# Top-k attention with a leaky-ReLU MLP: values and the scores of two units grouped on TensorE, with the PSUM banks shared out anew

## The chip, the cores and the metric

The kernel runs on one core of a Trainium2 chip. The metric is the device time of one execution in microseconds (us); lower is better. The engines are called PE (TensorE matmul), PEld (TensorE weight load), DVE (VectorE), ACT (ScalarE), POOL (GpSimd) and SP (SyncE, which here only issues DMAs).

## The reference

A batch of 8, with 8 heads, 576 tokens and head size 64, goes through attention in which each query keeps only its 32 largest scores. The result is laid out as 4608 tokens of 512 numbers and goes through an MLP of width 2048 with a leaky ReLU. All is in float32.

```python
scores = scale * np.matmul(q, k.transpose(0, 1, 3, 2))          # (8, 8, 576, 576)
kth = np.partition(scores, -top_k, axis=-1)[..., -top_k:-top_k + 1]   # top_k = 32
scores = np.where(scores >= kth, scores, -1000000000.0)
attn = np.exp(scores - np.max(scores, axis=-1, keepdims=True))
attn = attn / (np.sum(attn, axis=-1, keepdims=True) + 1e-09)
x = np.matmul(attn, v).transpose(0, 2, 1, 3).reshape(8 * 576, 512)
h = x @ w_in                                                    # (512, 2048)
g = np.maximum(0.01 * h, h)
return g @ w_out                                                # (2048, 512)
```

## The kernel before

**Units.** Attention is cut into 144 units. A whole unit is 128 queries of a pair of heads; its tile of scores is 128 x 2 x 576, one row of 576 for each query and each head. The 64 queries that 576 leaves over after four times 128 are taken from two pairs at once (a left unit, two per batch). A pair's two heads lie in partitions 0 to 63 and 64 to 127 of `qt` and `kt`, so a scores matmul uses half of the rows of the array.

**Steps.** The program is a list of steps, and every engine runs its instructions in the order in which the steps write them (`tc.manual_schedule()`). In step s, unit s is in `top_k` on DVE (four rounds of MAX8 and MATCH_REPLACE8 on the halves' pairwise maxima and minima). Unit s - 1 is masked on POOL (`mask`) and goes through the exponential on ACT (`exponents`, then `sums`, tile `ze`). Unit s - 2 gets its reciprocal on DVE (`rz`, which needs `ze`), is normalized on ACT, split into 16-bit halves on ACT (`split`), written to DRAM (`apart`) and read back transposed by a DMA (`wT`, three buffers).

**The block.** At the end of every even step comes a block of attention on PE: `scores` of units s + 2 and s + 3 (line 191) and `weigh_values` of units s - 4 and s - 3 (line 276), with the copies out of PSUM on ACT (`s_sb`, line 207, and `x`, line 297). In the kernel before, the order is scores of the first new unit, values of the two old ones, scores of the second new unit:

```python
            for u in new[:1]:
                scores(u)
            if s % 2 == 0:
                po = ps_po.tile([P, 2, P], F32, name="po")
                ...
            for u in new[1:]:
                scores(u)
```

A unit's scores are four matmuls of 288 columns for a whole unit (two heads, two halves of the keys), eight for a left unit. They go to two PSUM tiles of two banks each, `psc0` for one head and `psc1` for the other, and there is one buffer of each.

**The MLP.** Between the blocks PE works on the MLP of finished tokens, in chunks of 256 (two of 128 at first). `mlp(ch)` is a generator: first 16 chunks f of the hidden width, each of four matmuls of 256 columns into a tile `ph` with a Prelu on ACT into `gT[f]` (lines 330 to 340); then, per 128 tokens, 16 matmuls of 512 columns into a tile `pz`, a copy to `o_sb` and the DMA out. Every `yield` names the cost of what was issued, and `mlp_steps(budget)` takes pieces until a seventh of the step's share of the backlog is used; there are seven such calls in a step. The two early chunks of 128 tokens take another way (`hidden_of_few`), with x as the weights and PE transposes (`pt`) afterwards.

**PSUM.** There are eight banks: two each for `psc0` and `psc1`, one for `po` (the values), three for the MLP's tiles (`ps_ml`, tag "ml").

**Start.** The MLP's weights come in 16 pieces as 64-bit numbers, and `round_weights` makes float32 of each from its 16-bit words, over ACT, DVE and PE. Its PE sums use `psc0` and `psc1` in turn, and the last three pieces the MLP's banks. For odd pieces the step that makes `scale` (line 127) is on ACT, for even ones on DVE (line 131). The scores of units 0 and 1 are issued while the last pieces are under way.

Of the kernel before, what the change touches and what calls it, by code (L numbers as in the profile page):

```python
# [8 lines left out]
F32 = mybir.dt.float32  # L9
# [10 lines left out]
def kernel(  # L20
# [13 lines left out]
    nc = tc.nc  # L34
# [9 lines left out]
    HP = DMODEL // P  # L44
    B = NPAIR // HP
    HS = S // 2
    NFC = DFF // P
    WCH = 1024
    LEFT = S % P
# [11 lines left out]
    small = ctx.enter_context(tc.tile_pool(name="small", bufs=5))  # L61
    halves = ctx.enter_context(tc.tile_pool(name="halves", bufs=3, space=bass.MemoryType.DRAM))
    ps_sc = ctx.enter_context(tc.tile_pool(name="ps_sc", bufs=1, space=bass.MemoryType.PSUM))
    ps_po = ctx.enter_context(tc.tile_pool(name="ps_po", bufs=1, space=bass.MemoryType.PSUM))
    ps_ml = ctx.enter_context(tc.tile_pool(name="ps_ml", bufs=3, space=bass.MemoryType.PSUM))

    ident = const.tile([P, P], F32, name="ident")
    make_identity(nc, ident)
# [4 lines left out]

    w_in = [const.tile([P, DFF], F32, name=f"w_in{c}") for c in range(HP)]
    w_out = [const.tile([P, 4, DMODEL], F32, name=f"w_out{c}") for c in range(NFC // 4)]
    gT = [const.tile([P, CHMAX], F32, name=f"gT{f}") for f in range(NFC)]

# [23 lines left out]
    def round_weights(n):  # L103

        raw = raw_of.pop(n)
        dst = piece(n)  # L110
        mid = raw[:, :, 2]
        low = raw.rearrange("p n w -> p (n w)").bitcast(U32).rearrange("p (n w) -> p n w", w=2)[:, :, 0]
        top = raws.tile([P, WCH], U16, name="top", bufs=2)
        scale = raws.tile([P, WCH], U16, name="scale", bufs=2)
        parts = work.tile([P, 2 * NKC - 1, P], F32, name="wT", bufs=3)
        parts = parts.rearrange("p c n -> p (c n)").bitcast(U16)
        m_top, m_low = parts[:, 0:WCH], parts[:, WCH:2 * WCH].bitcast(BF16)
        nc.scalar.copy(top, raw[:, :, 3])
        nc.scalar.activation(dst, mid, AF.Copy, bias=-7.0 - 2.0 ** -16, scale=2.0 ** -20)

        nc.scalar.activation(m_low, low, AF.Copy, bias=128.0, scale=2.0 ** -29)  # L121
        yield
        nc.vector.tensor_scalar(scale, top, 4, 0x7FF, ALU.logical_shift_right, ALU.bitwise_and)

        nc.vector.tensor_scalar(scale, scale, 1151.0, 896.0, ALU.min, ALU.max)
        if n % 2:
            nc.scalar.activation(scale, scale, AF.Copy, bias=-896.0 * 128, scale=128.0)  # L127
        nc.vector.tensor_scalar(m_top, top, 0xF, 0x3F80, ALU.bitwise_and, ALU.bitwise_or)
        nc.vector.tensor_scalar(top, top, 0x8000, None, ALU.bitwise_and)
        if n % 2 == 0:  # L130
            nc.vector.tensor_scalar(scale, scale, 896.0, 128.0, ALU.subtract, ALU.mult)
        if n < NPIECE - 3:
            pw = ps_sc.tile([P, 2, 512], F32, name=f"psc{n % 2}")
            sums = [(pw[:, h, :], h * 512) for h in range(2)]
            ends = [(pw.rearrange("p h n -> p (h n)"), 0)]
        else:
            ends = sums = [(ps_ml.tile([P, 512], F32, name="pw", tag="ml"), h * 512) for h in range(2)]
        for pw, c in sums:
            at = slice(c, c + 512)
            nc.tensor.matmul(pw, ident_top, m_top[:, at].bitcast(BF16), start=True, stop=False)  # L140
            nc.tensor.matmul(pw, ident, dst[:, at], start=False, stop=False)
            nc.tensor.matmul(pw, ident_low, m_low[:, at], start=False, stop=True)
        yield
        nc.vector.tensor_tensor(scale, scale, top, ALU.bitwise_or)  # L144
        for pw, c in ends:
            at = slice(c, c + pw.shape[-1])
            nc.vector.tensor_tensor(dst[:, at], pw, scale[:, at].bitcast(BF16), ALU.mult)  # L147
# [40 lines left out]
                for hp in range(0, HP, 2)]  # L188
        units += left + whole if first else whole + left

    def scores(u):
        ps = [ps_sc.tile([P, 2, 512], F32, name=f"psc{i}") for i in range(2)]
        for n in range(0, len(u.parts), 2):
            for half in range(2):
                for i, pi, side, r0 in u.parts[n:n + 2]:
                    qt, kt = qk_of[pi]
                    d = slice(side * D, (side + 1) * D)
                    nc.tensor.matmul(  # L198
                        ps[i][r0:r0 + u.rows, half, 0:HS],
                        qt[d, u.q0:u.q0 + u.rows],  # L200
                        kt[d, half * HS:(half + 1) * HS],
                        start=True, stop=True,
                    )
        u.both = work.tile([P, 2, S], F32, name="s_sb", bufs=5)
        u.s = [u.both[:, i, :] for i in range(2)]
        for i in range(2):
            nc.scalar.copy(u.s[i].rearrange("p (h n) -> p h n", h=2), ps[i][:, :, 0:HS])  # L207

    def top_k(u):

# [90 lines left out]
    def hidden_of_few(x):  # L301

        g_of = {}
        for j in range(NFC // 4 + 1):
            if j < NFC // 4:
                ph = ps_ml.tile([P, 512], F32, name="ph", tag="ml")
                for c in range(HP):
                    nc.tensor.matmul(ph, x[c][:, 0:P], w_in[c][:, j * 512:(j + 1) * 512],  # L308
                                     start=(c == 0), stop=(c == HP - 1))
                    if c == 1:  # L310
                        yield 2 * 512
                g_of[j] = raws.tile([P, 2 * DMODEL], U16, name="scale", bufs=2).bitcast(F32)
                nc.scalar.activation(g_of[j], ph, AF.Prelu, alpha=SLOPE)
                yield 2 * 512
            if j:
                pt = ps_ml.tile([P, 4, P], F32, name="pt", tag="ml")
                for i in range(4):
                    nc.tensor.transpose(pt[:, i, :], g_of[j - 1][:, i * P:(i + 1) * P], ident)
                for i in range(4):
                    nc.scalar.copy(gT[4 * (j - 1) + i][:, 0:P], pt[:, i, :])  # L320
                yield 2 * P

    def mlp(ch):

        n = CHUNKS[ch]
        t0 = sum(CHUNKS[:ch])
        x = x_of[ch]
        if ch < EARLY:
            yield from hidden_of_few(x)
        for f in range(NFC if ch >= EARLY else 0):  # L330
            ph = ps_ml.tile([P, 512], F32, name="ph", tag="ml")
            for c in range(HP):
                nc.tensor.matmul(  # L333
                    ph[:, 0:n], w_in[c][:, f * P:(f + 1) * P], x[c][:, 0:n],
                    start=(c == 0), stop=(c == HP - 1),
                )
                if c == 1:
                    yield 2 * max(n, 225)
            nc.scalar.activation(gT[f][:, 0:n], ph[:, 0:n], AF.Prelu, alpha=SLOPE)  # L339
            yield 2 * max(n, 225)  # L340
        for r0 in range(0, n, P):
            m = min(P, n - r0)
            pz = ps_ml.tile([P, 512], F32, name="pz", tag="ml")
            for f in range(NFC):
                nc.tensor.matmul(  # L345
                    pz[0:m, 0:DMODEL], gT[f][:, r0:r0 + m], w_out[f // 4][:, f % 4, :],
                    start=(f == 0), stop=(f == NFC - 1),
                )
                if f % 2 and f + 1 < NFC:
                    yield 2 * DMODEL  # L350
            o_sb = work.tile([P, DMODEL], F32, name="o_sb", bufs=1)
            nc.scalar.copy(o_sb[0:m], pz[0:m, 0:DMODEL])
            nc.sync.dma_start(out[t0 + r0:t0 + r0 + m, :], o_sb[0:m])
            yield 2 * DMODEL
# [61 lines left out]
    with tc.manual_schedule():  # L416
# [12 lines left out]
        for n in range(NPIECE + 2):  # L429
            for i in (n, n - 1, n - 2) if AS_WORDS else ():  # L430
                if 0 <= i < NPIECE:
                    if i == n:
                        rounding[i] = round_weights(i)
                    next(rounding[i], None)
            load_weights(n + 3)
            if 6 <= n < 6 + HP:
                load_qk(n - 6)
            elif n == NPIECE - 1:
                for u in steps[0:2]:
                    scores(u)  # L440
            if n == NPIECE - 1:
                load_v(0)
                load_v(1)

        for s in range(len(steps) + LAG + 1):
# [29 lines left out]
            if old:  # L475
                exponents(old, 1)
                sums(old)
            for u in new[:1]:
                scores(u)
            if s % 2 == 0:  # L480
                po = ps_po.tile([P, 2, P], F32, name="po")
                for values in (weigh_values, keep_values):
                    for n, u in enumerate((unit(s - LAG - 1), unit(s - LAG))):
                        if u:
                            values(u, po[:, n, :])
                attended(s)
            for u in new[1:]:
                scores(u)
            budget = slot_budget(s + 1)
            mlp_steps(budget)  # L490
            mlp_steps(budget)
# [60 lines left out]
```

## Time and profile before

| What | Value |
|---|---|
| time, median of 3 runs | 1514.51 us (1513.94 to 1515.4) |
| span of the profiled execution | 1512.7 us |
| instructions | 24128 |
| scores on PE (L198) | x1280, 198.5 us busy |
| values on PE (L283) | x3200, 182.7 us busy |
| Prelu on ACT (L339), 128 x 256 | x272, 380 ns each |
| copies of the scores on ACT (L207), 128 x 576 | x288, 639 ns each |
| split on ACT (L259) | x288, 1144 ns each |

A row of the profile names the line of the kernel, the engine, the operation and its tiles as out<-in. "Busy" is the time in which at least one instruction of the row ran on the engine. A float32 matmul of the program stands as two instructions. Matmuls are pipelined and their ends are modelled, so their starts are the better measure, and a PE that shows as busy may still be slower than it could be. In a timeline the columns are the start, the length and the engine, then the line, the operation, the tiles and shapes and the count; a wait and what ended it stand in square brackets. "SPq" is the queue of SP, where DMAs are issued.

### The profile page before, as it was taken

What the parts mean: (1) busy time and instruction counts of PE and PEld (TensorE: products, weight loads), DVE (VectorE), ACT (ScalarE), POOL (GpSimd) and SP (SyncE); (2) the same over time, 40 slices, a digit from 0 to 9 for tenths busy, and PEclk for the clock granted to TensorE, in tenths of its full rate; (3) what the DMA queues carried; (4) which work ended last, traced back from release to release, by engine and by line L of the source; (5) the groups of instructions that cost most, each with busy time, mean ns of one, the idle gap of its engine ahead of it and who ended that gap; (6) DMA issues with size and microseconds to landing.
All of it is one profiled execution on the core that took longest, in us unless ns stands there. A gap on an engine that the chain in (4) does not pass through costs nothing.

```text
span 1512.7 us, 24128 instructions
## 1 busy us (share of the span) xinstructions
PE 1429.0 (94%) x8030; PEld 934.5 (62%) x8032; DVE 1330.4 (88%) x3421; ACT 1121.5 (74%) x2149; POOL 1079.5 (71%) x726
## 2 busy tenths in 40 slices
PE   5736988999999999999999999999999999999998
PEld 2314545767676766676767676767666766666774
DVE  6899899999999999899999998999999989999600
ACT  7846887878787877787878787878787777787720
POOL 0058788887878777778787787878887878788700
PEclk9965999999999999999999999999999999999999
DMA  7714466655655556656664565645755555555510
GB/s 283 282 31 125 119 169 182 161 139 143 186 154 151 128 164 158 174 126 156 173 169 137 141 159 168 171 132 149 186 157 150 134 158 154 151 140 136 140 52 14
DMA packets 399293, 227.03 MB, mean 150 GB/s; under 512 B 343360, under 2 KB 343360, under 8 KB 397120
## 3 DMA queue, kind: packets, MB, share of 16 engines
q1 hardware_dynamic: 399168, 225.49, 54.2%
q8 instruction: 63, 1.03, 0.3%
q14 instruction: 62, 0.51, 0.1%
HBM read 46.14 MB, written 94.37 MB: 93 GB/s over the span
## 4 chain that ended last, share of the span: by engine, by line
PE 84%; DVE 10%; ACT 3%; DMA 2%; issue 1%; SPq 0%; DVEq 0%; ACTq 0%
PE pz L345 31%; PE ph L333 31%; PE psc L198 10%; PE po L283 10%; DVE tops L221 4%; DVE pairs L224 3%; DMA wT<-apart 1%; DVE pairs L216 1%; PE ph L308 1%; DVE scale L144 1%; ACT split L259 1%; ACT scale L127 0%; ACT wT L121 0%; DVE w_in L147 0%; ACT s_sb L238 0%
## 5 line engine op out<-in xcount | busy, mean ns | idle before, releaser
L234 POOL TENSOR_SCALAR pen<-s_sb,tops 128x576 f32<-128x576 f32 x288 | 638.4, 2217 | 234.8 <-DVE tops L221 205.9
L221 DVE MAX8 tops<-pairs 128x8 f32<-128x288 f32 (+1 forms) x1152 | 635.8, 591 | 0.0
L345 PE MATMUL pz<-w_out,gT 128*128 128x512 f32 x1152 | 506.7, 595 | 0.0
L333 PE MATMUL ph<-x,w_in 128*128 128x256 f32 x2176 | 482.4, 381 | 0.0
L224 DVE MATCH_REPLACE8 pairs<-tops,pairs 128x288 f32<-128x288 f32 (+1 forms) x864 | 460.0, 537 | 0.0
L333 PEld LDWEIGHTS ph<-x,w_in 128*128 128x128 f32 x2176 | 408.9, 190 | 77.1 <-issue 19.8
L235 POOL TENSOR_TENSOR s_sb<-s_sb,pen 128x576 f32<-128x576 f32 x288 | 406.9, 1413 | 24.0
L345 PEld LDWEIGHTS pz<-w_out,gT 128*128 128x128 f32 x1152 | 215.9, 190 | 264.4 <-issue 263.5
L259 ACT COPY split<-s_sb 128x1152 uint16<-128x1152 uint16 x288 | 315.7, 1144 | 0.0
L207 ACT COPY s_sb<-psc 128x576 f32<-128x576 f32 x288 | 169.4, 639 | 108.9 <-PE psc L198 108.9
L250 ACT ACTIVATE s_sb<-s_sb,rz 128x576 f32<-128x576 f32 x288 | 206.7, 767 | 33.0 <-DVE rz L247 33.0
L238 ACT ACTIVATE s_sb<-s_sb,nbias 128x576 f32<-128x576 f32 x288 | 221.4, 769 | 11.5 <-POOL s_sb L235 11.5
L198 PE MATMUL psc<-kt,qt 64*128 64x288 f32 (+1 forms) x1280 | 198.5, 438 | 29.3 <-ACT s_sb L207 29.1
L216 DVE TENSOR_TENSOR pairs<-s_sb 128x576 f32<-128x576 f32 x288 | 213.7, 780 | 10.2 <-ACT split L259 0.5
L283 PE MATMUL po<-wT,vt 128*64 128x128 f32 (+1 forms) x3200 | 182.7, 271 | 22.7 <-DMA wT<-apart 22.7
L283 PEld LDWEIGHTS po<-wT,vt 128*64 128x64 f32 x3200 | 163.2, 140 | 54.7 <-issue 26.9
L198 PEld LDWEIGHTS psc<-kt,qt 64*128 64x128 f32 (+1 forms) x1280 | 110.9, 180 | 102.2 <-ACT s_sb L207 38.8
L339 ACT ACTIVATE gT<-ph 128x256 f32<-128x256 f32 x272 | 99.0, 380 | 94.6 <-PE ph L333 94.3
L232 POOL TENSOR_SCALAR nbias<-tops 128x2 f32<-128x2 f32 x144 | 33.5, 233 | 92.5 <-DVE tops L221 79.7
L247 DVE RECIPROCAL rz<-ze 128x2 f32<-128x2 f32 x144 | 22.4, 155 | 72.0 <-ACT ze L243 71.4
L297 ACT COPY x<-po 128x128 f32<-128x128 f32 (+1 forms) x160 | 32.5, 264 | 60.0 <-PE po L283 59.7
L224 DVE MATCH_VALUE_LOAD pairs<-tops,pairs 128x8 f32 x864 | 62.2, 72 | 0.0
(44 smaller groups left out, 378.3 us busy)
## 6 DMA issues: line engine op xcount, KB each, us to landing
apart<-split SPq DMA_DIRECT2D x288, 288.0 KB, 2.1
raw<-in_weights_dram SPq DMA_DIRECT2D x16, 1024.0 KB, 5.3
vt<-in_vk_dram SPq DMA_DIRECT2D x32, 320.0 KB, 3.6
qt<-in_qT_dram SPq DMA_DIRECT2D x32, 288.0 KB, 3.6
kt<-in_kT_dram SPq DMA_DIRECT2D x32, 288.0 KB, 4.1
out_dram<-o_sb SPq DMA_DIRECT2D x36, 256.0 KB, 2.0
wT<-apart SPq DMA_TRANSPOSE x144, 4.6
```

The source lines that it names most:

```text
L198: nc.tensor.matmul(ps[i][r0:r0 + u.rows, half, 0:HS], qt[d, u.q0:u.q0 + u.rows], kt[d, half * HS:(half + 1) * HS], start=True, stop=True,)
L216: nc.vector.tensor_tensor(pairs[:, :, n, :], u.both[:, :, 0:HS], u.both[:, :, HS:S], op)
L221: nc.vector.max(out=u.tops[:, i, r, :], in_=rest[i])
L224: nc.vector.match_replace(out=rest[i], in_to_replace=u.tops[:, i, r, :], in_values=rest[i], imm_value=LOWEST)
L234: nc.gpsimd.tensor_scalar(pen, u.s[i], u.tops[:, i, ROUNDS - 1, 7:8], MASKED, ALU.is_lt, ALU.mult)
L235: nc.gpsimd.tensor_tensor(u.s[i], u.s[i], pen, ALU.add)
L238: nc.scalar.activation(u.s[i], u.s[i], AF.Exp, bias=u.nbias[:, i:i + 1], scale=SCALE, accum_out=u.z[:, i:i + 1])
L250: nc.scalar.activation(u.s[i], u.s[i], AF.Copy, bias=0.0, scale=u.rz[:, i:i + 1])
L259: nc.scalar.copy(split, pairs[:, :, h])
L283: nc.tensor.matmul(po[side * D:(side + 1) * D, o, :], vt[:, c, side, :], u.wT[:, c + side * NKC if c + 1 < NKC else c, r:r + n], start=(c ...
L333: nc.tensor.matmul(ph[:, 0:n], w_in[c][:, f * P:(f + 1) * P], x[c][:, 0:n], start=(c == 0), stop=(c == HP - 1),)
L345: nc.tensor.matmul(pz[0:m, 0:DMODEL], gT[f][:, r0:r0 + m], w_out[f // 4][:, f % 4, :], start=(f == 0), stop=(f == NFC - 1),)
```

## The change

The block's order becomes values, then the scores of both new units in one run. For that the six banks beside the MLP's become one pool of three tiles of two banks: `wide`, with two buffers, and `narrow`, with one. A unit's 576 score columns are cut in 352 and 224 and no longer in two halves of 288. The 352 of each head go to a `wide` tile of the unit's own, and the 224 of both units share `narrow`. The run goes through the parts in the order first unit wide, first unit narrow, second unit narrow, second unit wide, and all the matmuls are issued before the copies on ACT. The values take a `wide` tile too, the one that the second unit's wide scores take after them.

The MLP gives up one bank and has two. Two chunks f of the hidden width now share a bank (`ph` is 128 x 2 x 256) and one Prelu. `gT` becomes one tile, so that a Prelu can write two chunks of it, and a copy in `hidden_of_few` four. In `round_weights` the last piece's scale goes to DVE.

What it is for: PE changes less often between kinds of matmul, the second unit's scores need not wait until the first unit's have left PSUM, and ACT has fewer instructions.

```diff
+    NARROW = 224
+    WIDE = S - NARROW
...
-    ps_po = ctx.enter_context(tc.tile_pool(name="ps_po", bufs=1, space=bass.MemoryType.PSUM))
-    ps_ml = ctx.enter_context(tc.tile_pool(name="ps_ml", bufs=3, space=bass.MemoryType.PSUM))
+    ps_ml = ctx.enter_context(tc.tile_pool(name="ps_ml", bufs=2, space=bass.MemoryType.PSUM))
...
-    gT = [const.tile([P, CHMAX], F32, name=f"gT{f}") for f in range(NFC)]
+    gT = const.tile([P, NFC, CHMAX], F32, name="gT")
...
-        if n % 2:
+        if n % 2 and n + 1 < NPIECE:
             nc.scalar.activation(scale, scale, AF.Copy, bias=-896.0 * 128, scale=128.0)
+        else:
+            nc.vector.tensor_scalar(scale, scale, 896.0, 128.0, ALU.subtract, ALU.mult)
...
-            pw = ps_sc.tile([P, 2, 512], F32, name=f"psc{n % 2}")
+            pw = ps_sc.tile([P, 2, 512], F32, name="wide", bufs=2)
...
-    def scores(u):
-        ps = [ps_sc.tile([P, 2, 512], F32, name=f"psc{i}") for i in range(2)]
-        for n in range(0, len(u.parts), 2):
-            for half in range(2):
+    def scores(us):
+        narrow = ps_sc.tile([P, 2, 512], F32, name="narrow")
+        ps = {}
+        for k, u in enumerate(us):
+            wide = ps_sc.tile([P, 2, 512], F32, name="wide", bufs=2)
+            ps[u] = ((wide[:, :, 0:WIDE], 0, WIDE),
+                     (narrow[:, :, k * NARROW:(k + 1) * NARROW], WIDE, S))
+        order = ((us[0], 0), (us[0], 1), (us[1], 1), (us[1], 0))
+        for u, part in order:
+            to, k0, k1 = ps[u][part]
+            for n in range(0, len(u.parts), 2):
                 for i, pi, side, r0 in u.parts[n:n + 2]:
...
+                    nc.tensor.matmul(to[r0:r0 + u.rows, i, :], qt[d, u.q0:u.q0 + u.rows],
+                                     kt[d, k0:k1], start=True, stop=True)
...
-        for i in range(2):
-            nc.scalar.copy(u.s[i].rearrange("p (h n) -> p h n", h=2), ps[i][:, :, 0:HS])
+        for u, part in order:
+            to, k0, k1 = ps[u][part]
+            nc.scalar.copy(u.both[:, :, k0:k1], to)
...
-                for i in range(4):
-                    nc.scalar.copy(gT[4 * (j - 1) + i][:, 0:P], pt[:, i, :])
+                nc.scalar.copy(gT[:, 4 * (j - 1):4 * j, 0:P], pt)
...
+        for f0 in range(0, NFC if ch >= EARLY else 0, 2):
+            ph = ps_ml.tile([P, 2, CHMAX], F32, name="ph", tag="ml")
+            for i in range(2):
+                f = f0 + i
+                for c in range(HP):
+                    nc.tensor.matmul(
+                        ph[:, i, 0:n], w_in[c][:, f * P:(f + 1) * P], x[c][:, 0:n],
+                        start=(c == 0), stop=(c == HP - 1),
+                    )
+                    if c == 1 or i == 0 and c == HP - 1:
+                        yield 2 * max(n, 225)
+            nc.scalar.activation(gT[:, f0:f0 + 2, 0:n], ph[:, :, 0:n], AF.Prelu, alpha=SLOPE)
             yield 2 * max(n, 225)
...
-            for u in new[:1]:
-                scores(u)
             if s % 2 == 0:
-                po = ps_po.tile([P, 2, P], F32, name="po")
+                po = ps_sc.tile([P, 2, 512], F32, name="wide", bufs=2)[:, 0, 0:2 * P].rearrange("p (u n) -> p u n", u=2)
...
-            for u in new[1:]:
-                scores(u)
+            if new:
+                scores(new)
```

More of the change, by code (lines that the diff above doesn't have):

```diff
@@ L125, in round_weights @@
         nc.vector.tensor_scalar(scale, scale, 1151.0, 896.0, ALU.min, ALU.max)
-        if n % 2:
+        if n % 2 and n + 1 < NPIECE:
             nc.scalar.activation(scale, scale, AF.Copy, bias=-896.0 * 128, scale=128.0)
+        else:
+            nc.vector.tensor_scalar(scale, scale, 896.0, 128.0, ALU.subtract, ALU.mult)
         nc.vector.tensor_scalar(m_top, top, 0xF, 0x3F80, ALU.bitwise_and, ALU.bitwise_or)
         nc.vector.tensor_scalar(top, top, 0x8000, None, ALU.bitwise_and)
-        if n % 2 == 0:
-            nc.vector.tensor_scalar(scale, scale, 896.0, 128.0, ALU.subtract, ALU.mult)
         if n < NPIECE - 3:
-            pw = ps_sc.tile([P, 2, 512], F32, name=f"psc{n % 2}")
+            pw = ps_sc.tile([P, 2, 512], F32, name="wide", bufs=2)
             sums = [(pw[:, h, :], h * 512) for h in range(2)]
@@ L197, in scores @@
                     d = slice(side * D, (side + 1) * D)
[L198 to L205, printed above, removed]
-        for i in range(2):
-            nc.scalar.copy(u.s[i].rearrange("p (h n) -> p h n", h=2), ps[i][:, :, 0:HS])
+                    nc.tensor.matmul(to[r0:r0 + u.rows, i, :], qt[d, u.q0:u.q0 + u.rows],
+                                     kt[d, k0:k1], start=True, stop=True)
+        for u in us:
+            u.both = work.tile([P, 2, S], F32, name="s_sb", bufs=5)
+            u.s = [u.both[:, i, :] for i in range(2)]
+        for u, part in order:
+            to, k0, k1 = ps[u][part]
+            nc.scalar.copy(u.both[:, :, k0:k1], to)
     def top_k(u):
@@ L329, in mlp @@
             yield from hidden_of_few(x)
[L330 to L339, printed above, removed]
+        for f0 in range(0, NFC if ch >= EARLY else 0, 2):
[10 more added lines that the diff above has]
+            nc.scalar.activation(gT[:, f0:f0 + 2, 0:n], ph[:, :, 0:n], AF.Prelu, alpha=SLOPE)
             yield 2 * max(n, 225)
@@ L345, in mlp @@
                 nc.tensor.matmul(
-                    pz[0:m, 0:DMODEL], gT[f][:, r0:r0 + m], w_out[f // 4][:, f % 4, :],
+                    pz[0:m, 0:DMODEL], gT[:, f, r0:r0 + m], w_out[f // 4][:, f % 4, :],
                     start=(f == 0), stop=(f == NFC - 1),
@@ L438 @@
             elif n == NPIECE - 1:
-                for u in steps[0:2]:
-                    scores(u)
+                scores(steps[0:2])
             if n == NPIECE - 1:
@@ L486 @@
                 attended(s)
-            for u in new[1:]:
-                scores(u)
+            if new:
+                scores(new)
             budget = slot_budget(s + 1)
```

## The prediction

> **What bounds the kernel now.** I read the page first (busy times, the slices, the chain), then the busy times of one long stretch, then the PE timeline of single blocks, then the waits.
>
> ```profile
> PE 1429.0 (94%) x8030; PEld 934.5 (62%) x8032; DVE 1330.4 (88%) x3421; ACT 1121.5 (74%) x2149; POOL 1079.5 (71%) x726
> ...
> PE   5736988999999999999999999999999999999998
> ...
> DVE  6899899999999999899999998999999989999600
> ...
> PE 84%; DVE 10%; ACT 3%; DMA 2%; issue 1%; SPq 0%; DVEq 0%; ACTq 0%
> PE pz L345 31%; PE ph L333 31%; PE psc L198 10%; PE po L283 10%; DVE tops L221 4%; DVE pairs L224 3%; DMA wT<-apart 1%; DVE pairs L216 1%; PE ph L308 1%; DVE scale L144 1%; ACT split L259 1%; ACT scale L127 0%; ACT wT L121 0%; DVE w_in L147 0%; ACT s_sb L238 0%
> ```
>
> The slices show three stages: a start in which PE has holes (to about 250 us), a long middle in which PE and DVE are both full, and a tail of MLP alone. The chain belongs to PE. Busy times of the middle:
>
> ```profile
> 260.00:1416.00 1156.00, 1154.37 (x6812) 780.64 (x6810) 1088.28 (x2832) 903.75 (x1775) 922.48 (x616) 1.00 0.57 153
> ```
>
> The order is PE, PEld, DVE, ACT, POOL, clock. PE has 1.6 us of holes in 1156, DVE 67.7 us. PE sets the pace; DVE could go 6% faster. A block of attention comes every second step; here is one, on PE:
>
> ```profile
> 801.06 14.08 PE L333 MATMUL ph<-x,w_in 128*128 128x256 f32 x64
> 815.08 1.24 PE L198 MATMUL psc<-kt,qt 64*128 64x288 f32 x8
> 816.25 2.40 PE L283 MATMUL po<-wT,vt 128*64 128x128 f32 x40
> 818.58 1.24 PE L198 MATMUL psc<-kt,qt 64*128 64x288 f32 x8
> 819.75 2.86 PE L333 MATMUL ph<-x,w_in 128*128 128x256 f32 x12
> ```
>
> Start to start: scores 1.17, values 2.33, scores 1.17 us, the rest of a period of about 18.7 us (1156 us hold 62) is MLP. A matmul of the program stands as two instructions. A later block differs in one place:
>
> ```profile
> 1021.71 1.24 PE L198 MATMUL psc<-kt,qt 64*128 64x288 f32 x8
> 1022.88 2.40 PE L283 MATMUL po<-wT,vt 128*64 128x128 f32 x40
> 1025.21 1.61 PE L198 MATMUL psc<-kt,qt 64*128 64x288 f32 x8
> 1026.75 3.50 PE L333 MATMUL ph<-x,w_in 128*128 128x256 f32 x15
> ```
>
> The second scores take 1.54 us here. ACT was late and had not emptied psc1 of the first unit, so one row group of the array ran alone for a while. PE counts as busy all through it, so no wait shows.
>
> **What the Trainium skill says.** "TensorEngine Tiling (Array Packing)", Tiling Modes, Key Properties: a change of tiling mode drains the engine. The trace fits. The MLP's 64 instructions of 256 columns take 14.02 us start to start, 0.86 ns a column. A scores run streams 8 x 288 columns in two row groups side by side, so 4 x 288 x 0.86 = 0.99 us, and takes 1.17: 0.18 us of each run is fixed (the drain and the first weight load, which nothing hides). "PSUM — Partial Sum Buffer", PSUM bank collisions: engines are kept apart by bank, not by address. So the copy of one unit's narrow half must wait until the other unit's narrow half, in the same bank, is written; no run here shows that yet. "ScalarE: Activation LUTs", What ACT_TABLE_LOAD costs: an ACTIVATE has a fixed part and 0.833 ns an element, so merging two saves one fixed part. The trace agrees: 0.38 us for 256 columns, 0.60 for the early chunks' 512.
>
> **The change part by part.**
>
> 1. *Scores of two units in one run, after the values.* Columns are unchanged: 4 x 352 + 4 x 224 = 2304 column times in two row groups, 1.97 us, plus 0.18 fixed: 2.15 us for what took 2.34. The narrow matmuls (0.19 us) are about as long as a weight load (median 186 ns at L198), so loads stay hidden; were they not, four of them would lose 0.03 us each. Gain 0.19 us a block, 62 blocks, all on the path: 11.8 us.
>
> 2. *No wait for the first unit's copies between the two scores.* Reading the second scores runs of all 62 blocks on the timeline, 12 take 1.54 and two 1.39 us in place of 1.17, and single ones more at batch borders: 12 x 0.37 + 2 x 0.22, about 5 us, which I take as gained.
>
> 3. *The new wait: the second unit's wide scores take the slot of the values,* so they wait for ACT to copy both x halves (0.43 us). Behind that waiting matmul stand all of PE's later MLP matmuls. PE has first the first unit's wide and both narrow halves to do: 2 x 0.30 + 4 x 0.19 and 0.10 of the start, 1.46 us. ACT, when punctual, is done about 0.55 us after the scores start (copy at 818.70 for 0.43 us, scores at 818.58). When late, its last step before (ze) ends up to 1.6 us after the values start (at 1024.46 against 1022.88), with the values then starting 1.17 us after the block; in the new order this is 2.8 us against values of 2.33, so 0.45 us later: done at 1.0 us. Cost nil, hidden by the scores ahead of it; the upper bound is a few tenths in few blocks.
>
> 4. *Values move ahead of the first scores, 1.17 us earlier in the block.* They need wT, which comes by split, DMA, transpose.
>
> ```profile
> 1018.29 2.26 SPq L262 DMA_TRANSPOSE wT<-apart  x1
> ...
> L262 SPq DMA_TRANSPOSE wT<-apart x144: 2223/2555/3607, 107.6 to 1443.9; - x144
> ...
> DMA to landing us min/median/max: 4.3/4.6/6.4
> ```
>
> That transpose lands at about 1022.8, and the values' second unit starts at half of its run, 1024.0: 1.1 us to spare. Doing so for all blocks, a third have 1.0 to 1.4 us, most others 1.7 to 3.0, eight less than 1. Taken 1.17 us earlier, the eight lose 0.3 to 1.1 us each, 6.6 us in all, the next third about nothing. ACT's lighter load (part 5) helps a little: I take 6 us lost; the bounds are 2 and 15 us.
>
> 5. *MLP in pairs of f chunks, two banks in place of three.* ACT: 136 x (2 x 0.38 - 0.60) = 22 us less, off the path. PE: same matmuls. A bank must be empty one fill later, 16 x 0.216 = 3.45 us, as before two fills of 1.73 later. Today's Prelus end up to 3.2 us (at worst 3.7) after their matmuls, since norm, exp and split (1.43 + 0.96 + 2.2 us) stand ahead; there will be half as many. Cost nil, at worst some tenths in a quarter of the pairs, 5 us. The 32 gT copies of the early chunks become 8, on ACT in the start.
>
> 6. *Start.*
>
> ```profile
> 75.69 1.07 ACT L127 ACTIVATE scale<-scale 128x1024 uint16<-128x1024 uint16 x1
> ...
> 76.80 0.69 DVE L144 TENSOR_TENSOR scale<-scale,top 128x1024 uint16<-128x1024 uint16 x1 [2.53 <-ACT scale L127]
> 77.59 1.29 DVE L147 TENSOR_TENSOR w_out<-pw,scale 128x512 f32<-128x512 f32 x2
> 78.80 1.41 DVE L216 TENSOR_TENSOR pairs<-s_sb 128x576 f32<-128x576 f32 x2
> ```
>
> The last piece's scale waits on ACT behind the copies of the scores; the change does it on DVE. Scores then end at 71.32 + 2.15 = 73.5, the last piece's matmuls (2.68 us) at 76.2, and half of L147 later DVE starts top_k at about 76.9, not 78.8: 1.9 us, on DVE's chain. Some of the 4.8 us that DVE waits for ACT at 150 to 170 (ACT there waits for PE, which comes late out of its scores) goes too, 1.5 us. Together 3.4 us; it could be nothing, or 6. Tail: values without scores, nothing gained.
>
> Sum: 11.8 + 5 + 3.4 - 6 = 14.2 us. 1514.5 - 14.2 = 1500 us.
>
> **The rivals.**
> (a) *The gain goes back to the transposed weights.* PE is faster, but the way from DVE's last round over POOL's mask, exp, split and two DMAs to the values is not, so the values wait for whatever PE gained. For: spare time of 1 us in a third of the blocks. Against: the others have 2 to 3 us, and ACT idles for PE (93.6 us at L207, 70.1 at L339, 45.9 at L297 in the middle). Only the start is gained: 1511 us.
> (b) *Slower.* Values wait in most blocks and Prelus of pairs come late: 0.4 us of waiting in each of 62 blocks for wT and 0.2 for ACT is 37 us against 20 gained (11.8 + 5 + 3.4): 1531 us. With half of those waits the change would be worth nothing. Against: ACT gets lighter, and PE waited for gT for 4.3 us in all.
> (c) *More.* ACT's 22 us come as earlier splits, values never wait, DVE's 58.6 us of waiting for ze shrinks: parts 1, 2 in full with the batch borders (6.6) and a start of 6 us: 1514.5 - 11.8 - 6.6 - 6 = 1490 us.
>
> **How the numbers follow.** The forecast 0.60, (a) 0.12, (b) 0.08, (c) 0.20. Half of (a) lies within 0.2% (3 us). Faster: 0.60 + 0.20 + 0.06 = 0.86, same 0.06, slower 0.08. The range goes from a little under (c), 1487, to (a), 1512. It leaves out (b), part of (a) and a tail below.
>
> **What would show it.** In the changed profile a block on PE should read values 2.33 us, then 16 scores instructions in 2.15 us with nothing between. A longer scores run means part 3's wait. PE's waits for wT in the middle (1.5 us before) should sum to 2 to 15 us; more is (a). The Prelu should show at 0.60 us x136, the first pairs<-s_sb near 76.9 us. The period should fall from 18.7 to about 18.5 us with DVE's share up from 94 to 95%. I am wrong if PE's stretch between blocks grows (banks), or if holes for wT appear in most blocks.

## The result, and the profile after

| | before | after |
|---|---|---|
| time, median of 4 runs each | 1514.95 us (1513.94 to 1516.49) | 1508.01 us (1506.74 to 1509.66) |
| span of the profiled execution | 1512.7 us | 1507.3 us |

The ratio is 0.9954, 95% interval 0.9937 to 0.9971: 7 us faster, within the range, and half of the 14.2 us forecast. From the changed kernel's page, its busy times, two rows of its slices and its chain:

```profile
PE 1401.8 (93%) x8032; PEld 930.3 (62%) x8032; DVE 1334.2 (89%) x3422; ACT 1111.3 (74%) x1988; POOL 1078.3 (72%) x726
...
PE   5625877999999999999999999999999999999998
...
DVE  6899799999999999999999999999999999999600
...
PE 79%; DVE 9%; DMA 5%; ACT 5%; issue 1%; SPq 0%; DVEq 0%; ACTq 0%
```

PE is busy for 27 us less, and the span is only 5.4 us shorter, so PE waits more than it did. The second to seventh of the 40 slices each show one tenth less PE, the full ones none: the waits are in the first 260 us. The chain has DMA and ACT at 5% each, 2% and 3% before. Next, the busy times of the stretch from 260 to 1416 us (in the order PE, PEld, DVE, ACT, POOL, clock), and the PE timeline of one block:

```profile
260.00:1416.00 1156.00, 1150.69 (x6917) 793.71 (x6918) 1103.61 (x2871) 906.03 (x1669) 933.98 (x624) 1.00 0.56 155
```

```profile
802.86 14.08 PE L343 MATMUL ph<-x,w_in 128*128 128x256 f32 x64
816.87 2.46 PE L292 MATMUL wide<-wT,vt 128*64 128x128 f32 x40
819.26 0.86 PE L209 MATMUL wide<-kt,qt 64*128 64x352 f32 x4
819.96 0.92 PE L209 MATMUL narrow<-kt,qt 64*128 64x224 f32 x8
820.72 0.76 PE L209 MATMUL wide<-kt,qt 64*128 64x352 f32 x4
821.40 2.86 PE L343 MATMUL ph<-x,w_in 128*128 128x256 f32 x12
```

The middle is as the forecast drew it. The stretch holds 105 more PE instructions than before, and DVE went from 1088 to 1104 us in it. In the block the 16 scores instructions take 821.40 - 819.26 = 2.14 us with nothing between them; the MLP goes on at full pace (64 instructions in 14.01 us).

To see where the time goes, I cut PE's timeline into runs of values, scores and MLP, each from its start to the start of the next, waits included. The ninth run of values stands where the start ends; there are 72 in either kernel.

| us | before | after | difference |
|---|---|---|---|
| up to the start of the ninth values run | 270.5 | 280.4 | +9.9 |
| from there to the start of the last | 1179.0 | 1163.7 | -15.3 |
| of which scores | 147.95 | 131.04 | -16.9 |
| of which values | 150.48 | 153.39 | +2.9 |
| of which MLP | 880.57 | 879.27 | -1.3 |
| after it | 63.2 | 63.2 | 0 |

So nothing went wrong in the middle. The start, for which the forecast had a gain of 3.4 us, lost 9.9. DVE sets the pace of the start (between 60 and 270 us over half of the chain that ended last is DVE's in the kernel before), so its timeline dates the loss, by the beginning of top_k for each unit (the rows `pairs<-s_sb`). After, then before:

```profile
80.54 1.42 DVE L225 TENSOR_TENSOR pairs<-s_sb 128x576 f32<-128x576 f32 x2
...
163.45 1.52 DVE L225 TENSOR_TENSOR pairs<-s_sb 128x576 f32<-128x576 f32 x2
170.18 0.17 DVE L256 RECIPROCAL rz<-ze 128x2 f32<-128x2 f32 x1 [2.06 <-ACT ze L252]
179.61 2.64 DVE L225 TENSOR_TENSOR pairs<-s_sb 128x576 f32<-128x576 f32 x2 [5.17 <-ACT s_sb L216]
...
190.16 1.52 DVE L225 TENSOR_TENSOR pairs<-s_sb 128x576 f32<-128x576 f32 x2
```

```profile
162.26 1.52 DVE L216 TENSOR_TENSOR pairs<-s_sb 128x576 f32<-128x576 f32 x2
167.87 0.17 DVE L247 RECIPROCAL rz<-ze 128x2 f32<-128x2 f32 x1 [0.94 <-ACT ze L243]
172.22 1.45 DVE L216 TENSOR_TENSOR pairs<-s_sb 128x576 f32<-128x576 f32 x2
181.02 1.52 DVE L216 TENSOR_TENSOR pairs<-s_sb 128x576 f32<-128x576 f32 x2
```

The first top_k begins at 80.54 us, not 78.80, so 1.7 us are lost with the weights. At 163 us the delay is still 1.2. Then DVE stands for 5.17 us without scores to work on; by the unit after that, 190.16 against 181.02, the delay is 9.1 us. The PE timeline of the changed kernel shows what held both up:

```profile
66.28 0.38 PE L143 MATMUL pw<-wT,ident_low 128*128 128x512 bf16 x1
70.69 0.38 PE L141 MATMUL pw<-wT,ident_top 128*128 128x512 bf16 x1 [4.03 <-DVE w_out L148]
...
72.58 1.91 PE L142 MATMUL pw<-w_out,ident 128*128 128x512 f32 x2
...
74.85 1.01 PE L209 MATMUL wide<-kt,qt 64*128 64x352 f32 x4
...
164.05 0.66 PE L327 MATMUL pt<-ident,scale 128*128 128x128 f32 x4 [0.25 <-ACT scale L322]
168.71 6.40 PE L355 MATMUL pz<-w_out,gT 128*128 128x512 f32 x8 [4.00 <-ACT gT L328]
175.04 2.40 PE L292 MATMUL wide<-wT,vt 128*64 128x128 f32 x40
177.38 0.86 PE L209 MATMUL wide<-kt,qt 64*128 64x352 f32 x4
```

Two waits of 4 us, both for a bank of the MLP. At 70.69 the sums of the last but one weight piece wait until DVE has emptied the piece before, which holds both banks; the first scores stand behind them on PE and start at 74.85, where before they started at 71.32 (the PE timeline of before):

```profile
71.32 1.24 PE L198 MATMUL psc<-kt,qt 64*128 64x288 f32 x8
```

At 168.71 the first `pz` waits until ACT has emptied one of the last two `pt` tiles, and behind `pz` stand the values and then the scores that DVE waits for. In ACT's timeline, again of the changed kernel, those copies come last:

```profile
163.40 0.60 ACT L322 ACTIVATE scale<-ph 128x512 f32<-128x512 f32 x1 [3.31 <-PE ph L317]
163.90 1.43 ACT L259 ACTIVATE s_sb<-s_sb,rz 128x576 f32<-128x576 f32 x2
165.23 0.76 ACT L247 ACTIVATE s_sb<-s_sb,nbias 128x576 f32<-128x576 f32 x1
165.90 0.19 ACT L247 ACTIVATION_READ_ACCUMULATOR s_sb<-s_sb,nbias 128x1 f32 x1
165.99 2.19 ACT L268 COPY split<-s_sb 128x1152 uint16<-128x1152 uint16 x2
168.08 1.06 ACT L328 COPY gT<-pt 128x512 f32<-128x512 f32 x2
```

The normalization, an exponential and the split of other units stand between the last Prelu (163.40) and these copies; `pz` starts when the first of the two is done. In the kernel before, the copies of the last two `pt` were as far behind, but PE had a third bank (the PE and the ACT timeline of before):

```profile
161.38 0.66 PE L318 MATMUL pt<-ident,scale 128*128 128x128 f32 x4 [0.25 <-ACT scale L313]
161.87 3.60 PE L345 MATMUL pz<-w_out,gT 128*128 128x512 f32 x8
```

```profile
165.41 1.43 ACT L320 COPY gT<-pt 128x128 f32<-128x128 f32 x8
```

Here `pz` starts 0.5 us after the last transposes and 3.5 us ahead of the copies.

### The profile page after: what moved, and what is told of

Read it like the earlier page. It is cut to its first block, busy times and chain, and to the rows that moved or that the text cites. A ratio compares the mean times of both kernels' runs of the same rounds, so it can differ in the third digit from the quotient of the medians.

```text
span 1507.3 us, 24058 instructions
## 1 busy us (share of the span) xinstructions
PE 1401.8 (93%) x8032; PEld 930.3 (62%) x8032; DVE 1334.2 (89%) x3422; ACT 1111.3 (74%) x1988; POOL 1078.3 (72%) x726
## 3 DMA queue, kind: packets, MB, share of 16 engines
q8 instruction: 63, 1.03, 0.3%
## 4 chain that ended last, share of the span: by engine, by line
PE 79%; DVE 9%; DMA 5%; ACT 5%; issue 1%; SPq 0%; DVEq 0%; ACTq 0%
PE pz L355 29%; PE ph L343 29%; PE wide L292 10%; PE wide L209 6%; DVE tops L230 4%; PE narrow L209 3%; DVE pairs L233 3%; DMA wT<-apart 2%; DMA apart<-split 2%; ACT split L268 2%; DVE pairs L225 1%; ACT s_sb L259 1%; ACT s_sb L247 1%; PE ph L317 1%; DMA raw<-in_weights_dram 1%
## 5 line engine op out<-in xcount | busy, mean ns | idle before, releaser
L292 PE MATMUL wide<-wT,vt 128*64 128x128 f32 (+1 forms) x3200 | 184.2, 271 | 61.6 <-DMA wT<-apart 60.5
L292 PEld LDWEIGHTS wide<-wT,vt 128*64 128x64 f32 x3200 | 163.6, 140 | 105.0 <-ACT s_sb L247 35.0
L306 ACT COPY x<-wide 128x128 f32<-128x128 f32 (+1 forms) x160 | 32.2, 260 | 153.5 <-PE wide L292 153.5
L349 ACT ACTIVATE gT<-ph 128x512 f32<-128x512 f32 x136 | 80.7, 594 | 80.9 <-PE ph L343 80.9
L216 ACT COPY s_sb<-wide 128x704 f32<-128x704 f32 x144 | 108.7, 755 | 30.6 <-PE wide L209 30.5
L209 PE MATMUL wide<-kt,qt 64*128 64x352 f32 (+1 forms) x640 | 120.8, 496 | 0.4 <-ACT x L306 0.4
L216 ACT COPY s_sb<-narrow 128x448 f32<-128x448 f32 x144 | 69.6, 535 | 4.0 <-PE narrow L209 3.3
L209 PE MATMUL narrow<-kt,qt 64*128 64x224 f32 (+1 forms) x640 | 70.0, 360 | 0.2 <-DMA kt<-in_kT_dram 0.2
```

The source lines that it names most:

```text
L209: nc.tensor.matmul(to[r0:r0 + u.rows, i, :], qt[d, u.q0:u.q0 + u.rows], kt[d, k0:k1], start=True, stop=True)
L292: nc.tensor.matmul(po[side * D:(side + 1) * D, o, :], vt[:, c, side, :], u.wT[:, c + side * NKC if c + 1 < NKC else c, r:r + n], start=(c ...
```

## The experiments

The theories, by the letters of the texts on record. A: two banks in place of three make the start late, through the weight sums and through `hidden_of_few`; the middle doesn't feel them. B: the order does, since in the start the values wait for `wT` and the scores now stand behind them. B', a later form: of the loss, the 2.8 us that A's cures leave come from the order, and putting both scores ahead of the values for the first 20 steps would win them back. Times are medians; the kernel before took 1515.1 to 1515.5 us in the runs beside them. "Start" is the ninth values run, "middle" the time from there to the last.

**A bank more for the start, two ways (e1, e2, e3).** The `pt` tiles of `hidden_of_few` go to a `wide` buffer (e1), one weight piece's sums go to `narrow` (e2), or both (e3).

```diff
-                pt = ps_ml.tile([P, 4, P], F32, name="pt", tag="ml")
+                pt = ps_sc.tile([P, 2, 512], F32, name="wide", bufs=2)[:, 0, :].rearrange("p (i n) -> p i n", i=4)
```

```diff
-        if n < NPIECE - 3:
-            pw = ps_sc.tile([P, 2, 512], F32, name="wide", bufs=2)
+        if n < NPIECE - 2:
+            pw = (ps_sc.tile([P, 2, 512], F32, name="wide", bufs=2) if n < NPIECE - 3
+                  else ps_sc.tile([P, 2, 512], F32, name="narrow"))
```

> The changed kernel with one edit: the transposes of the two early chunks (pt) write to a wide tile, so the MLP's two banks hold only ph and pz there. Theory A (the start is later because the MLP has two banks instead of three, above all in the two early chunks): the wait of 4.0 us of pz for the gT copies and the waits of ph L317 go, the ninth values run starts about 6 to 8 us earlier than at 280.4 us, time about 1501. Theory B (the start is later because the scores now stand behind values that wait for transposed weights): nothing changes, about 1508.

> The changed kernel with one edit: the sums of the third last weight piece go to the narrow tile instead of the MLP's two banks, so the second last piece finds both of these free. Theory A: PE's wait of 4.0 us for w_out at 66 us goes, the first pairs<-s_sb on DVE comes at about 77 instead of 80.5 us, and, as DVE is full until 128 us, the ninth values run comes some 2 to 3 us earlier, time about 1505. If the moved scale step or the scores' order were the cause of the late 80.5 us, it stays.

> Both edits in one. Theory A: the gains add up, the start is no longer later than before (ninth values run at 270 us or a little earlier) and the middle keeps its 15 us, so about 1498 us, faster than both kernels. Theory B: about 1505 to 1508.

| | time | ratio to before | start | middle |
|---|---|---|---|---|
| the change | 1508.01 | 0.9954 (0.9937 to 0.9971) | 280.4 | 1163.7 |
| e1, `pt` in `wide` | 1504.49 | 0.9925 (0.9910 to 0.9940) | 275.7 | 1162.7 |
| e2, one piece in `narrow` | 1504.96 | 0.9929 (0.9915 to 0.9944) | 276.8 | 1162.6 |
| e3, both | 1500.85 | 0.9901 (0.9885 to 0.9918) | 273.3 | 1162.1 |

They take 4.7 and 3.6 us off the start, and together 7.1 of the 9.9; the forecast for e3 was all of it. The PE timeline of e3 where the change had its 4.00 us:

```profile
160.10 0.66 PE L328 MATMUL wide<-ident,scale 128*128 128x128 f32 x4 [0.25 <-ACT scale L323]
160.59 3.60 PE L356 MATMUL pz<-w_out,gT 128*128 128x512 f32 x8
164.76 2.40 PE L293 MATMUL wide<-wT,vt 128*64 128x128 f32 x40 [0.57 <-ACT gT L329]
...
216.75 4.54 PE L293 MATMUL wide<-wT,vt 128*64 128x128 f32 x40 [3.54 <-ACT gT L329]
```

The wait is gone, and a smaller one has come with the loan: at 216.75 the values need a `wide` buffer that the second early chunk's `pt` still holds, 3.54 us. e3 is 14 us faster than the kernel before and 7 us faster than the change.

**Pairs of f chunks alone, with three banks and with two (e7, e8).** The kernel before, its tiles and order kept, gets the paired Prelu and the single `gT`; e8 also has two MLP banks.

```diff
-        for f in range(NFC if ch >= EARLY else 0):
-            ph = ps_ml.tile([P, 512], F32, name="ph", tag="ml")
...
-            nc.scalar.activation(gT[f][:, 0:n], ph[:, 0:n], AF.Prelu, alpha=SLOPE)
+        for f0 in range(0, NFC if ch >= EARLY else 0, 2):
+            ph = ps_ml.tile([P, 2, CHMAX], F32, name="ph", tag="ml")
...
+            nc.scalar.activation(gT[:, f0:f0 + 2, 0:n], ph[:, :, 0:n], AF.Prelu, alpha=SLOPE)
```

```diff
-    ps_ml = ctx.enter_context(tc.tile_pool(name="ps_ml", bufs=3, space=bass.MemoryType.PSUM))
+    ps_ml = ctx.enter_context(tc.tile_pool(name="ps_ml", bufs=2, space=bass.MemoryType.PSUM))
```

> The kernel before with one edit: Prelus in pairs (ph of 128 x 2 x 256 in one bank) and gT as one tile; three MLP banks, the old tiles and the old order. What the pairs alone are worth: start unchanged (ninth values run at 270.5 us), the MLP and the values in the middle some 2 to 4 us shorter, since ACT has 22 us less, time about 1511 to 1514.

> As the run with pairs and three banks, but with two MLP banks. Theory A: the ninth values run comes 6 to 8 us later (277 to 279 us) with the old order and the old tiles, the middle stays, time 6 to 8 us above the run with three banks. If the order alone made the start late, it stays at 270.5 us.

| | time | ratio to before | start | middle | its scores | its values | its MLP |
|---|---|---|---|---|---|---|---|
| before | 1514.95 | 1 | 270.5 | 1179.0 | 147.95 | 150.48 | 880.57 |
| e7, three banks | 1508.17 | 0.9958 (0.9944 to 0.9973) | 270.3 | 1171.4 | 142.47 | 149.65 | 879.27 |
| e8, two banks | 1519.03 | 1.0031 (1.0021 to 1.0041) | 283.2 | 1170.7 | 142.23 | 149.24 | 879.27 |

One line, `bufs=3` to `bufs=2`, moves the start by 12.9 us, more than the 6 to 8 expected, and the middle by -0.7. PE's waits between 60 and 285 us name the same two places in e8 (columns: wait in total, times, longest):

```profile
PE pz L347 <- ACT gT L320: 4.2, 1, 4.2
PE pw L140 <- DVE w_out L147: 2.7, 1, 2.7
```

This is theory A, shown with none of the new order in the kernel. e7 has `gT` as one tile too and does not start late, so what `pz` waits for under the name of `gT` is the bank that ACT empties into it, not the data of the one tile. The surprise is e7: the pairs alone bring 7 us, as much as the whole change. They took 5.5 us out of the scores, though the second unit's scores still had to wait for the first unit's copies. From the ninth values run on, those copies ended after the second scores had started in 15 of 61 blocks of the kernel before, and in none of e7, whose ACT has 136 Prelus where it had 272.

**The old order with the new tiles (e4).** Scores of one unit, values, scores of the other, from the changed kernel.

```diff
-        order = ((us[0], 0), (us[0], 1), (us[1], 1), (us[1], 0))
+        order = [(u, part) for u in us for part in range(2)]
...
+            if new:
+                scores(new[:1])
...
-                scores(new)
+                scores(new[1:])
```

> The changed kernel with the old order of the block: scores of one unit, values, scores of the other, all else as changed (two banks for the MLP, paired Prelus, parts of 352 and 224). From the ninth values run to the last, the two scores runs should take 2 x 1.17 us or more in place of 2.14, so that stretch is 12 to 17 us longer than 1163.7 us. Theory A: the start stays late (ninth values run near 280 us), time about 1520 or more. Theory B: the start goes back to 270 us, time about 1510.

1517.0 us, ratio 1.0011 (1.0002 to 1.0019): 9 us more than the change. The middle is 1171.6, scores 143.57 (12.5 more) and values 148.76 (4.6 less), so the grouping is worth 7.9 us there. The start is 282.1: with the old order it is no earlier than with the new, so the order is not what made it late, and B falls.

**Both scores ahead of the values in the start (e5, e6).** e5 is the change, e6 is e3, each with

```diff
+            if new and s < 20:
+                scores(new)
...
-            if new:
+            if new and s >= 20:
                 scores(new)
```

> The changed kernel with one edit: in the blocks before step 20 both scores come ahead of the values, so they don't stand behind values that wait for wT. Theory A (two banks alone make the start late): no change, ninth values run at 280 us, time about 1508. Theory B' (of the 9.9 us by which the start is later, 2.8 that the bank edits left come from this order, which also leaves PE idle and its clock at half for the scores): ninth values run at about 277 to 278 us, time about 1505.

> The changed kernel with the transposes in wide, the third last weight piece in narrow, and the scores ahead of the values before step 20. Theory A with B': the ninth values run comes at 270 to 271 us as in the kernel before, the stretch from there to the last values run stays at 1162 to 1164 us, time about 1498. Theory A alone: 273 us and 1501 as with the first two edits.

e5 took 1510.88 us, ratio 0.9972 (0.9964 to 0.9980), with the start at 285.4, 5 us later than with the change. PE's waits in e5, over the whole span:

```profile
PE wide L292 <- ACT s_sb L216: 36.7, 6, 14.0
...
PE pz L355 <- ACT gT L328: 4.0, 1, 4.0
```

The edit brings a wait of its own, which neither theory had: the values now need the `wide` buffer that the first unit's scores hold, and start only when ACT has copied it (the ACT, then the PE timeline of e5):

```profile
124.83 0.73 ACT L216 COPY s_sb<-wide 128x704 f32<-128x704 f32 x1
```

```profile
125.61 4.54 PE L292 MATMUL wide<-wT,vt 128*64 128x128 f32 x40 [13.95 <-ACT s_sb L216]
```

The 4.0 us of the bank stay. e6 took 1502.03 us, 0.9915 (0.9900 to 0.9930), with the start at 274.5; its time can't be told from that of e3. So this way of putting the scores first wins nothing back. It does not settle B', since with these tiles the new wait comes with it.

**The last piece's scale (e9, e10).** e9 is e3 with this step back on ACT, e10 the kernel before with this step alone moved to DVE (the first diff is e9's).

```diff
-        if n % 2 and n + 1 < NPIECE:
+        if n % 2:
             nc.scalar.activation(scale, scale, AF.Copy, bias=-896.0 * 128, scale=128.0)
```

```diff
-        if n % 2:
+        if n % 2 and n + 1 < NPIECE:
             nc.scalar.activation(scale, scale, AF.Copy, bias=-896.0 * 128, scale=128.0)
...
-        if n % 2 == 0:
+        if n % 2 == 0 or n + 1 == NPIECE:
             nc.vector.tensor_scalar(scale, scale, 896.0, 128.0, ALU.subtract, ALU.mult)
```

> The kernel with pt in `wide` and one weight piece in `narrow` (1500.85 us), and the last piece's scale back on ACT. Theory (forecast part 6): DVE's last scale step waits for ACT behind the copies of the scores; the first pairs<-s_sb comes at about 79.5 to 80.5 us instead of 78.3 and the time is 1 to 2 us longer, about 1502.5. Rival: with two MLP banks DVE is held at that place by PE's weight sums (pw waits 1.9 us for DVE), so the step on ACT is hidden: first pairs<-s_sb within 0.4 us of 78.3, time within 0.7 us of 1500.9.

> The kernel before with nothing changed but the last piece's scale on DVE. Theory (forecast part 6): DVE's wait of 2.53 us for ACT goes, DVE pays 0.43 us for the step itself; the first pairs<-s_sb comes at about 76.9 instead of 78.8 us, the ninth values run about 1.9 us earlier than 270.5, the time 1513.2. Rival 1: PE's sums of the last piece, behind the first scores, are the next limit, and first pairs<-s_sb comes at 78 or later; time 1514.5 to 1515.2. Rival 2: the gain at 78 us is lost later in the start: ninth values run at 270 to 271, time as before.

e9 took 1499.06 us, 0.9897 (0.9882 to 0.9913), not to be told from e3; e10 took 1514.76 us, 0.9995 (0.9986 to 1.0003). The DVE timeline of e10, then that of e9:

```profile
74.24 0.68 DVE L144 TENSOR_TENSOR scale<-scale,top 128x1024 uint16<-128x1024 uint16 x1
76.27 0.69 DVE L147 TENSOR_TENSOR w_out<-pw,scale 128x512 f32<-128x512 f32 x1 [1.35 <-PE pw L142]
77.50 0.69 DVE L147 TENSOR_TENSOR w_out<-pw,scale 128x512 f32<-128x512 f32 x1 [0.54 <-PE pw L142]
78.11 1.42 DVE L216 TENSOR_TENSOR pairs<-s_sb 128x576 f32<-128x576 f32 x2
```

```profile
75.88 0.69 DVE L146 TENSOR_TENSOR scale<-scale,top 128x1024 uint16<-128x1024 uint16 x1 [1.28 <-ACT scale L128]
76.67 1.29 DVE L149 TENSOR_TENSOR w_out<-pw,scale 128x512 f32<-128x512 f32 x2
77.88 1.42 DVE L226 TENSOR_TENSOR pairs<-s_sb 128x576 f32<-128x576 f32 x2
```

In e10 the wait for ACT is gone and one for PE's sums of that piece stands in its place; the first top_k came at 78.11, not 78.80, of which 0.3 us were already there before this step (the piece before began 0.28 us earlier), and the ninth values run at 271.8. So the step is worth 0.4 us where 1.9 were forecast, and nothing at the end. In e9 DVE waits for ACT again, 1.28 us, and the sums are there when it is done: the first top_k came even 0.4 us earlier than in e3.

## What was right and what was wrong in the prediction

- *Part 1, scores in one run: right.* 2.14 us a run where 2.15 was forecast. From e8 to the change, the scores of the middle fall by 11.2 us, against 11.8.
- *Part 2, no wait for the first unit's copies: right in size, but not the order's alone.* The waits are gone, but the pairs of part 5 take them away in the old order already (e7: scores 5.5 us shorter). The order without the pairs was not run. The pairs, booked as "off the path", were worth 7 us by themselves.
- *Part 3, the new wait for the `x` copies: right.* In the steady block the scores follow the values with no wait, and of the 61 runs of scores in the middle 59 take 2.10 to 2.14 us, the other two 2.32 and 2.57.
- *Part 4, values earlier: right in kind, too dear.* The values of the middle take 2.9 us more, against 6 (bounds 2 and 15); from e8, where ACT is light as well, it is 4.2. Of PE's waits there, those for `wT` grew by 1.0 us (2.5 against 1.5), and one of 1.1 us for a load of `vt` is new.
- *Part 5, two banks at no cost, at worst 5 us: wrong.* It holds for what I worked it out on, pairs of 256 columns in the middle: MLP 879.27 us with two banks and with three. But the banks also carry the sums of the last three weight pieces and the tiles of `hidden_of_few`, and for those the working had no term: the loss of a bank was put at nothing there. It cost 12.9 us with the old order and tiles (e8 against e7).
- *Part 6, the start at -3.4 us: wrong, and the step that decided.* It measured +9.9. Its working kept the first scores at 71.32 us, where the kernel before had them, with the last piece's sums right behind; no bank was waited for. They started at 74.85, after the wait of 4.03 us for a bank. The moved scale alone gives nothing (e10). In place of the 1.5 us to be gained at 150 to 170 us came the 4.00 us of PE waiting for a bank and the 5.17 us of DVE waiting for scores.

With -15.3 in the middle for the forecast -10.8 (the sum without part 6), and +9.9 for -3.4 at the start, the rest adds up: 14.2 + 4.5 - 13.3 = 5.4 us, the difference of the two spans. Rival (a), the gain given back, came nearer with its 1511 us, but by luck: it had waits for `wT` in the middle, and PE waits for them only 2.5 us between 285 and 1416 us. No rival had the banks in the start as what gives the gain back.

The page "Perfetto Trace Analysis" of the Trainium skill (Optimizing Tensor Performance, Matmuls) says that matmul groups should rotate through PSUM banks so that one is emptied while the next is filled. The traces here agree, and add where: two banks were as good as three in the middle, and made PE wait 4.00 us where ACT had 4.2 us of other units' work ahead of the copy (163.90 to 168.08). I had the ACT timeline of before in hand, with the last two `pt` emptied some 5 us after they were written; laying the list of everything that takes a bank beside it would have shown the wait.

What stays open: in e3 and e9 the start still ends 2 to 3 us later than in the kernel before (273.3 and 272.4 against 270.5). In e3 the last wait of values for `wT` ends at 254.02 us, before it ended at 251.95: 2.1 us. Behind those values stand the scores of two units, which take 3.81 us until the MLP goes on at 260.16; before it was one unit and 1.89 us, and the other unit's 1.17 us came after the MLP. That is 0.75 us more, and the two make up the 2.8. So a small part may be the order, as B' had it; this is read off the timelines, and no run shows it. Why `wT` lands later isn't shown either; the wait of 3.54 us at 216.75 may have a part in it, and no run took that one away.

## What to carry to other kernels

When a pool loses a buffer, list every kind of tile that goes through it, in every stage, and ask of each how long its reader is busy with other work; a pool that has room to spare in the steady state can be what holds up the start. Where buffers of another pool stand idle in that stage, as `narrow` and `wide` did here, lend one: two edits of a few words doubled what the change brought. And try the parts of a bundle alone, for merging the small instructions of an engine that is "off the path" can bring as much as the part that the change is named for (here 7 us for the pairs alone, 7.9 us of the middle for the grouping).

## What the runs showed that was not expected

After PE's wait of 4.03 us at 66 to 70 us its matmuls ran at full pace for 1.1 us and then at half: the float32 matmul of 512 columns at 72.58 (two instructions) took 1.91 us, the one at 70.91 took 1.03, and the mean granted clock was 0.68 between 72 and 77 us. DVE then waited 2.40 us for the sums of the last piece, which stood behind all this, so here a wait for a bank was paid twice. "TensorE: Matmul & The Clock Gate" (Part 1) says that an idle window of about 3.4 us halves the clock and a busy one restores it. This stretch fits. The kernel before does not: its granted clock was 0.50 from 64.3 to 67.6 us, after a wait of PE of only 2.38 us that had ended at 63.18. So in these traces the clock fell after a shorter wait too. There it cost little, for the next sums had to wait 1.04 us for DVE all the same.
